# A Mamba-2 scan with a low-rank mixer on one core: 56 TensorE transposes replaced by VectorE 32x32 transposes and a trip through DRAM

## Chip, core and metric

The kernel runs on one core of a Trainium2 chip. The metric is the device time of one execution in microseconds, the median of the runs. The profile is one more execution, taken by the hardware profiler. Its span runs from the first to the last instruction that the profile shows.

## What is computed

Inputs are x (4 batches, 8 heads, 768 steps, 32 channels), the decay a (4, 8, 768), B and C (4, 8, 768, 16), and the mixer's weights U (768 x 32), V (32 x 768), w_ch1 (256 x 1024), w_ch2 (1024 x 256). The reference, cut:

```python
for c in range(nc):                       # chunks of 32 steps
    cum = np.cumsum(la, axis=-1)          # la = log of the decays of the chunk
    L = np.exp(cum[..., :, None] - cum[..., None, :]) * causal
    M = np.einsum('bhin,bhjn->bhij', Cc, Bc) * L
    y_intra = np.einsum('bhij,bhjd->bhid', M, xc)
    y_inter = np.einsum('bhin,bhnd->bhid', Cc, state) * np.exp(cum)[..., None]
    y[:, :, sl] = y_intra + y_inter
    state = decay_full * state + sum over j of Bc[j] xc[j] decay_from_j[j]
x = y.transpose(0, 2, 1, 3).reshape(B, S, H * D)     # (4, 768, 256)
h = x.transpose(0, 2, 1) @ U @ V
u = x + h.transpose(0, 2, 1)
out = u + np.maximum(u @ w_ch1, 0.0) @ w_ch2
```

## The kernel before

The scan works on pairs k = 0 to 11 of two chunks of 128 steps; three pairs make a batch. The mixer works on blocks j = 0 to 2 of 256 steps of a batch. The order of all work is written out by hand: the string PLANS[1] holds words, and `follow` emits each word's instructions in turn, so every engine runs its own instructions in the order of the words. Engines wait for one another through semaphores alone. All DMAs are issued by SyncE (SP), also in order.

Words of the scan, with pair 3 + n for the word's number n (so T3 is pair 6, the first of batch 2, and t6 to t8 are batch 3):

- L loads B, C and x. P (`prep`) scales B and C on VectorE. D (`decayed`) scales B for the states.
- T (`turned`, which runs `turning`) transposes B and C: four TensorE transposes of 128x128 (L497) into one PSUM bank w, then three ACT operations: a copy to T (L501) and two masked copies to Cm (L507). A pair has two T words, each with two of the transposes.
- g (`gram`) multiplies Cm and T (L529), m and M mask the result on VectorE, s (`state`) makes the chunks' states (L564), u (`update`) chains them on VectorE and copies them masked to Sm on ACT (L596).
- n (`intra`, L684) and i (`inter`, L659) make y, channels by steps, in four PSUM banks; y (`yout`) copies it to yT in six ACT operations.
- t (`ytokens`) transposes y back to steps by channels: four TensorE transposes (L714) and a copy to ytok, on ACT for batches 0 and 1, on VectorE for 2 and 3.

Words of the mixer, with the lag of the batch first (p1 is batch 0, p0 batch 1, p-1 batch 2, p-2 batch 3):

- p (`project`, L748) multiplies ytok by U, x (`mixed`, L760) multiplies by V, and a (`added`) adds the result to yT on VectorE, which makes u. Batch 3's p-2 waits for t8, and all of batch 3's mixing waits for p-2.
- S (`split`) splits a block of u in three parts of the type fp32r: one ACT operation and two VectorE ones. f and e (L812 to 831) are the first matmul's two passes with a scaling and a Relu on ACT; h (`third`) makes two more parts on VectorE. R (`refined`) splits the weights in the same manner.
- d (`piece`) is one piece, four matmuls of 128x256, of the second matmul of a block. `down` adds u on VectorE at the end and stores the block: batches 1 to 3 by one VectorE transpose of 128x512 in 32x32 squares and four DMAs that put the squares where they belong (L907 to 912), batch 0 by four TensorE transposes (L920), an ACT copy and one DMA. Batch 3's last block goes through `rows`, whose u is transposed at its start by four TensorE transposes and one ACT copy (L848, L850), while its matmuls give steps by channels right away.

PSUM holds 2 banks w, 3 x and 3 z. A word that needs a bank waits until the bank's last reader is done.

Of the kernel before, what the change touches and what calls it, by code (L numbers as in the profile page):

```python
# [10 lines left out]
FP32 = mybir.dt.float32  # L11
# [3 lines left out]
WCOLS = 512  # L15
NWORDS = 12
PLAIN = 2
ROWS = 3
FOUR = 3

# [3 lines left out]
AF = mybir.ActivationFunctionType  # L24
# [19 lines left out]
        'U1.0.0 g0 U1.0.1 g1 m0 M0 c5 c4 m1 M1 c5 D1 s0 u0 U1.1.0 U1.1.1 U1.1.2 i0 n0 y0 c6 c6 '  # L44
        's1 c5 g2 c7 u1 R2 m2 c7 U1.1.3 M2 c8 c8 c7 U1.0.2 L4 U1.0.3 i1 n1 y1 c6 R1 R0 c8 R5 c9 '
        's2 c9 c9 n2 d1.0 L5 R6 u2 R0 d1.1 P3 S1.2 d1.0 R7 d1.0 i2 y2 R3 t1 R1 t0 R2 R5 d1.1 R4 '
        'f1.2.0 D4 T3 T3 P4 R7 R6 t2 f1.2.1 R3 D3 d1.1 f1.2.2 d1.0 R4 e1.2.0 d1.1 h1.2.0 e1.2.1 '
        'T4 f1.2.3 d1.0 T4 e1.2.2 e1.2.3 h1.2.1 P5 g3 p0 m3 M3 L6 d1.2 d1.2 d1.2 T5 L7 d1.2 L8 '
        'T5 h1.2.2 x0 h1.2.3 d1.2 a0.0 d1.2 d1.2 a0.1 S0.0 d1.2 g4 m4 s3 f0.0.1 D5 M4 f0.0.0 '
        'd1.2 d1.2 d1.2 e0.0.0 e0.0.1 u3 h0.0.0 f0.0.2 d1.2 h0.0.1 f0.0.3 e0.0.2 s4 u4 n3 h0.0.2 '  # L50
        'i3 e0.0.3 h0.0.3 d1.1 D6 S0.1 d1.2 d0.0 d0.0 y3 d0.0 d0.0 d0.0 S0.2 d0.0 d0.0 d0.0 D7 '
        'n4 s5 i4 d0.0 d0.0 g5 P7 y4 u5 P6 m5 M5 d0.0 d0.0 t3 D8 f0.2.1 f0.1.2 s6 n5 i5 y5 '
        'e0.1.2 u6 f0.2.0 f0.1.0 f0.1.3 h0.1.2 T7 e0.2.0 h0.2.0 e0.2.1 e0.1.3 h0.2.1 P8 T7 '
        'h0.1.3 f0.1.1 d0.2 f0.2.2 f0.2.3 e0.1.0 h0.1.0 e0.1.1 h0.1.1 e0.2.2 e0.2.3 h0.2.3 d0.1 '
        'd0.1 T6 T6 d0.1 d0.1 d0.1 t4 h0.2.2 t5 d0.1 d0.1 d0.1 d0.2 d0.2 d0.2 d0.2 d0.0 g7 m7 '
        'p-1 d0.2 d0.2 x-1 M7 a-1.0 a-1.1 s7 d0.2 u7 d0.1 d0.1 d0.1 g6 m6 d0.1 M6 d0.1 d0.2 d0.2 '
        'd0.2 d0.2 d0.2 S-1.0 T8 T8 i6 n6 y6 s8 n7 S-1.1 i7 y7 f-1.0.2 f-1.0.3 g8 e-1.0.2 '
        'e-1.0.3 m8 M8 f-1.1.0 f-1.0.1 h-1.0.3 h-1.0.2 f-1.0.0 f-1.1.1 e-1.1.0 e-1.0.0 e-1.0.1 '
        'h-1.1.0 h-1.0.1 e-1.1.1 f-1.1.2 h-1.0.0 d-1.0 S-1.2 f-1.1.3 e-1.1.2 h-1.1.2 d-1.0 d-1.0 '
        'd-1.0 d-1.0 f-1.2.0 u8 d-1.0 d-1.0 h-1.1.1 d-1.1 e-1.2.0 h-1.2.0 t6 e-1.1.3 f-1.2.2 '  # L60
        'd-1.1 d-1.1 d-1.0 h-1.1.3 e-1.2.2 h-1.2.2 d-1.1 d-1.1 d-1.1 d-1.1 d-1.1 i8 n8 t7 d-1.1 '
        'd-1.1 y8 d-1.1 t8 p-2 d-1.1 x-2 d-1.0 d-1.0 a-2.0 f-1.2.1 a-2.1 S-2.0 d-1.0 d-1.0 S-2.1 '
        'f-1.2.3 e-1.2.1 h-1.2.1 f-2.0.2 e-1.2.3 f-2.0.0 f-2.0.1 d-1.2 d-1.2 e-2.0.0 h-1.2.3 '
        'e-2.0.2 h-2.0.0 f-2.0.3 S-2.2 h-2.0.2 d-1.2 e-2.0.1 d-1.2 d-1.2 d-1.2 e-2.0.3 h-2.0.3 '
        'f-2.1.0 h-2.0.1 f-2.1.1 f-2.1.2 e-2.1.0 e-2.1.1 h-2.1.0 f-2.1.3 d-1.2 d-1.2 d-1.1 '
        'e-2.1.2 h-2.1.1 f-2.2.1 e-2.1.3 d-2.0 d-1.2 d-1.2 d-2.0 d-2.0 d-2.0 h-2.1.2 d-1.2 d-1.2 '
        'd-2.1 d-2.1 d-1.0 h-2.1.3 f-2.2.0 f-2.2.2 d-2.0 d-2.0 d-2.0 d-2.0 e-2.2.2 d-2.1 e-2.2.0 '
        'h-2.2.0 d-1.2 h-2.2.2 d-2.0 d-2.0 f-2.2.3 d-2.1 d-2.1 d-2.1 e-2.2.3 d-2.0 d-2.1 d-2.1 '
        'e-2.2.1 h-2.2.3 d-2.0 d-2.2 d-2.2 d-2.2 d-2.0 h-2.2.1 d-2.1 d-2.1 d-2.1 d-2.1 d-2.2 '
        'd-2.1 d-2.2 d-2.2 d-2.2 d-2.2 d-2.2 d-2.2 d-2.2 d-2.2 d-2.2 '),  # L70
}


# [1 line left out]
def kernel(  # L75
# [27 lines left out]
    nc = tc.nc  # L103
    P = 128
    NB, NH, S, D = x.shape
# [7 lines left out]
    NCB = DM // P  # L113
    HS = 2 * P
    VS = S // 2
    W = DF // 4
    NBL = S // HS
# [25 lines left out]
    def bank(tag, *dims):  # L143
        t = psum.tile([P, *dims], FP32, tag=tag, name=tag, bufs=BANKS[tag])
        if fills[0]:
            idle(t if len(dims) == 1 else t.rearrange(
                {2: "p a b -> p (a b)", 3: "p a b c -> p (a b c)"}[len(dims)]), fills[0])
        fills[0] = 0
        return t
# [39 lines left out]
    def hold(load, until):  # L189

        tc.add_manual_dep(load.ins, until.ins.name, mybir.DependencyInfo(
            mybir.DependencyClass.Sync, mybir.DependencyReason.DATA))
# [293 lines left out]
    def turning(k, c=0, n=2, tag="w", engine=None, sooner=False):  # L486

        s = st[k]
        if c == 0:
            s["T"] = att.tile([P, 2, 2, P], FP32, tag="T", name="T", bufs=3)  # L490
            s["Cm"] = att.tile([P, 2, 2, P], FP32, tag="Cm", name="Cm", bufs=3)
        tp = bank(tag, 2, n, P)
        for i in range(2):
            for v in range(n):
                if i or v:
                    yield
                nc.tensor.transpose(out=tp[:, i, v],  # L497
                                    in_=s["BC"][:, i, c + v].rearrange("p h n -> p (h n)"),
                                    identity=ident)
        if sooner or not engine:  # L500
            nc.scalar.copy(out=s["T"][:, :, c:c + n], in_=tp)  # L501
        for i in range(2):
            if engine:
                engine.tensor_scalar(out=s["Cm"][:, i, c:c + n], in0=tp[:, 1],
                                     scalar1=slot[:, i, None], scalar2=None, op0=ALU.mult)
            else:
                nc.scalar.activation(s["Cm"][:, i, c:c + n], tp[:, 1], AF.Copy,  # L507
                                     scale=slot[:, i, None])
        if engine and not sooner:
            nc.scalar.copy(out=s["T"][:, :, c:c + n], in_=tp)  # L510
        yield

    def turn(*args):
        for _ in turning(*args):
            pass
# [215 lines left out]
    def ytokens(*args):  # L731
        for _ in ytokening(*args):
            pass


    def mixer(b):
# [35 lines left out]
        def block(j):  # L772
            return uT[:, :, ts(j, HS)]
# [67 lines left out]
        def rows(j):  # L841

            u = raw.tile([P, 2 * WCOLS], INT32, tag="words", name="words", bufs=NWORDS).bitcast(
                FP32)[:, :HS // P * DM].rearrange("p (k n d) -> p k n d", n=NCB, d=P)
            t = bank("w", HS // P, NCB, P)
            for k in range(HS // P):
                for n in range(NCB):
                    nc.tensor.transpose(out=t[:, k, n], in_=block(j)[:, n, ts(k, P)],  # L848
                                        identity=ident)
            nc.scalar.copy(out=u, in_=t)  # L850
            yield
            o = mix.tile([P, 2 * WCOLS], FP32, tag="o", name="o")
            at = {}
            order = [(0, 0), (0, 1), (1, 0), (1, 1), (0, 2), (1, 2)]
            for k, v in order:
                if not v:
                    at[k] = bank("xz"[k % 2], DM)
                t = at[k]
                for half in range(2):
                    products(t, [(gs[j, m // 2][v][:, m % 2, ts(k, P)], w2[v][:, m])  # L860
                                 for m in range(NQ * half, NQ * half + NQ)], v + half == 0)
                    if v == 1 and half:
                        scaled(t)
                    if v == 2 and half:
                        vector.tensor_tensor(out=o[:, ts(k, DM)], in0=t,
                                             in1=u[:, k].rearrange("p n d -> p (n d)"),
                                             op=ALU.add)
                        nc.sync.dma_start(
                            out=out[b].rearrange("(j k p) m -> j k p m", j=NBL, p=P)[j, k],
                            in_=o[:, ts(k, DM)])  # L870
                    yield

        def down(j):
# [20 lines left out]
            else:  # L894
                for n in range(NCB):
                    for half in range(2):
# [4 lines left out]
                        if n and half:  # L901
                            added_to(t)
                        yield
            if b:
                o = mix.tile([P, 2 * WCOLS], FP32, tag="o", name="o")
                o = o[:, :NCB * HS].rearrange("p (n i) -> p n i", n=NCB)
                vector.transpose(out=o, in_=block(j))  # L907
                for r in range(4):
                    nc.sync.dma_start(
                        out=out[b, ts(j, HS)].rearrange(  # L910
                            "(k t) (n a c) -> a t n k c", t=Q, n=NCB, c=Q)[r],
                        in_=o[ts(r, Q)].rearrange("p n (k c) -> p n k c", c=Q))
                yield
                return
# [56 lines left out]

    def turned(k):

        t = turns.setdefault(k, turning(k))
        for _ in range(2):
            next(t)

    def crossed(k):

# [2 lines left out]
    def ytokens_of(k, v):  # L982
# [3 lines left out]

    scans = dict(P=prep, D=decayed, T=turned, g=gram, s=state, m=lambda k: mask(k, (0, 1)),
                 M=lambda k: mask(k, (2, 3)), u=update, i=lambda k: inter(k, 0), n=intra,
                 j=crossed, y=yout, t=ytokens, L=load, Q=lambda k, c: prep(k, c, 1),
                 E=lambda k, c: decayed(k, c, 1), O=ytokens_of,  # L990
                 V=lambda k, c, v: turn(k, c, 1, "wx"[v // 2 % 2], vector if v % 2 else None, v > 3))
    whole = dict(c=convert, R=refined, A=lambda i: decays(every_batch, "w", [i]),
# [56 lines left out]
```

## Time and profile before

| what | us |
|---|---|
| median of 3 runs (lowest, highest) | 219.41 (219.27, 221.42) |
| the profiled execution, its own time | 219.55 |
| its span | 217.8 |
| TensorE (PE) busy | 205.9 |
| weight loads (PEld) busy | 185.1 |
| VectorE (DVE) busy | 168.3 |
| ScalarE (ACT) busy | 125.0 |
| GpSimd (POOL) busy | 6.6 |

The page gives, for each engine, busy time, share of the span and number of instructions, then the span in 40 equal slices with the busy share of each in tenths. A group of instructions is a line of the kernel, an engine, an operation and the tiles written and read, with busy time and mean duration in ns, and the idle time just before them with what ended it. VectorE's instructions all carry L169, the line of a helper, and are told apart by their tiles. PE is the matmuls, PEld the weight loads that overlap them. A TensorE transpose counts as a matmul.

### The profile page before, as it was taken

To read this page: it belongs to the slowest core of one execution; us is meant where nothing else is said; L and a number is where in the kernel's file an instruction comes from. 1 tells how busy PE (TensorE), PEld (TensorE's weight loads), DVE (VectorE), ACT (ScalarE), POOL (GpSimd) and SP (SyncE) were. 2 spreads that over 40 slices of the span, in tenths; PEclk is the share of its full clock that TensorE was granted. 3 is DMA by queue.
4 is the path that set the end of the run, shared out by engine and by line. 5 is a ranking of instruction groups with operands and counts; after the bars stand their busy time and mean duration, and the time that the engine had idled before them with its cause. 6 is when DMAs were issued, how large, how long until landed. Compare 5 with 4: busy or idle time off the path is not lost.

```text
span 217.8 us, 7530 instructions
## 1 busy us (share of the span) xinstructions
PE 205.9 (95%) x3246; PEld 185.1 (85%) x3246; DVE 168.3 (77%) x349; ACT 125.0 (57%) x287; POOL 6.6 (3%) x22
## 2 busy tenths in 40 slices
PE   7778799999999999999999999979999999999994
PEld 5555586878879998999999988869999899999993
DVE  3398978998899998699858967847994597874871
ACT  3353749479969774368589513667563276635410
POOL 4132100000000000000000000000000000000000
PEclk9999969999999999999999999999999999999999
DMA  5996789986751017406600020330000000033234
GB/s 82 134 159 178 105 123 225 249 147 157 99 73 26 3 50 97 52 16 87 147 6 0 0 40 14 50 54 0 3 0 3 3 2 0 3 48 51 36 60 96
DMA packets 84016, 14.60 MB, mean 67 GB/s; under 512 B 80336, under 2 KB 82192, under 8 KB 83984
## 3 DMA queue, kind: packets, MB, share of 16 engines
q1 hardware_dynamic: 83984, 14.13, 37.0%
q8 instruction: 25, 0.41, 0.9%
q14 instruction: 7, 0.06, 0.1%
HBM read 10.98 MB, written 3.15 MB: 65 GB/s over the span
## 4 chain that ended last, share of the span: by engine, by line
PE 83%; DVE 6%; ACT 3%; SPq 2%; issue 2%; DMA 2%; POOL 1%; DVEq 0%
PE x L791 35%; PE z L791 28%; PE x L529 3%; SPq L195 2%; PE w L497 2%; PE w L748 2%; PE w L714 2%; DMA bc<-in_B_dram 2%; DVE words L169 2%; PE x L760 2%; PE x L684 1%; PE x L659 1%; PE w L564 1%; PE z L684 1%; DVE M L169 1%
## 5 line engine op out<-in xcount | busy, mean ns | idle before, releaser
L169 DVE SCALAR_TENSOR_TENSOR words<-words 128x512 fp32r<-128x512 f32 (+6 forms) x60 | 39.3, 667 | 4.3 <-PE x L791 1.4
L791 PE MATMUL x<-words,w 128*128 128x256 f32 x288 | 38.3, 280 | 0.0
L791 PEld LDWEIGHTS x<-words,w 128*128 128x128 f32 x288 | 34.9, 188 | 1.8 <-issue 1.7
L791 PE MATMUL z<-u,w 128*128 128x256 f32 x240 | 34.0, 280 | 1.3 <-issue 1.3
L791 PE MATMUL x<-u,w 128*128 128x256 f32 x240 | 34.0, 281 | 0.0
L791 PEld LDWEIGHTS z<-u,w 128*128 128x128 f32 x240 | 30.1, 188 | 1.6 <-issue 1.3
L791 PEld LDWEIGHTS x<-u,w 128*128 128x128 f32 x240 | 30.1, 188 | 0.6 <-issue 0.2
L796 ACT ACTIVATE z<-z 128x512 f32<-128x512 f32 (+1 forms) x24 | 13.9, 578 | 18.0 <-PE z L791 18.0
L796 ACT ACTIVATE x<-x 128x512 f32<-128x512 f32 (+1 forms) x27 | 15.4, 574 | 14.5 <-PE x L791 14.3
L169 DVE SCALAR_TENSOR_TENSOR words<-x,words 128x512 fp32r<-128x512 f32 x20 | 13.7, 685 | 10.7 <-ACT words L831 10.5
L791 PE MATMUL z<-words,w 128*128 128x256 f32 x144 | 19.3, 280 | 0.0
L791 PEld LDWEIGHTS z<-words,w 128*128 128x128 f32 x144 | 17.5, 188 | 0.4 <-issue 0.4
L831 ACT ACTIVATE words<-z 128x512 fp32r<-128x512 f32 x20 | 11.8, 601 | 6.1 <-PE x L791 4.3
L831 ACT ACTIVATE words<-x 128x512 fp32r<-128x512 f32 x20 | 11.8, 600 | 4.8 <-PE x L791 4.7
L169 DVE SCALAR_TENSOR_TENSOR words<-z,words 128x512 fp32r<-128x512 f32 x20 | 13.6, 679 | 1.2 <-ACT words L831 1.2
L169 DVE SCALAR_TENSOR_TENSOR S<-S,kept,w 128x64 f32<-128x64 f32 x40 | 11.2, 279 | 1.6
L169 DVE TENSOR_TENSOR BC<-bc,F 128x512 f32<-128x512 f32 (+2 forms) x18 | 8.9, 508 | 4.2 <-DMA bc<-in_B_dram 2.8
L169 DVE TENSOR_TENSOR M<-x,causal 128x256 int32<-128x256 int32 x24 | 9.0, 417 | 3.8 <-PE z L529 3.8
L169 DVE TENSOR_TENSOR yT<-x,yT 128x384 f32<-128x384 f32 (+1 forms) x15 | 9.2, 612 | 3.2 <-PE z L760 3.1
L596 ACT ACTIVATE Sm<-S,slot 128x128 f32<-128x128 f32 (+1 forms) x18 | 6.1, 386 | 9.1 <-DVE S L169 9.1
L529 PE MATMUL x<-Cm,T 32*64 32x128 f32 x192 | 9.4, 307 | 1.7 <-DVE Cm L169 1.7
L659 PE MATMUL z<-T,Sm 32*64 32x64 f32 x180 | 7.7, 239 | 2.1 <-DVE settled L169 2.0
(152 smaller groups left out, 377.5 us busy)
## 6 DMA issues: line engine op xcount, KB each, us to landing
words<-in_moe_w_ch_dram SPq DMA_DIRECT2D x7, 512.0 KB, 5.9
x<-in_x_dram SPq DMA_DIRECT2D x24, 128.0 KB, 3.9
out_dram<-o SPq DMA_DIRECT2D x32, 64.0 KB, 2.2
bc<-in_B_dram SPq DMA_DIRECT2D x24, 64.0 KB, 3.3
bc<-in_C_dram SPq DMA_DIRECT2D x12, 128.0 KB, 3.7
out_dram<-words SPq DMA_DIRECT2D x3, 256.0 KB, 3.2
words<-in_moe_w_ch_dram SPq DMA_DIRECT2D x2, 256.0 KB, 4.8
out_dram<-o SPq DMA_DIRECT2D x2, 128.0 KB, 1.8
```

Of the source, the lines that this page charges most:

```text
L169: self.last = call(*args, **kwargs)
L195: op = nc.sync.dma_start(**kwargs)
L497: nc.tensor.transpose(out=tp[:, i, v], in_=s["BC"][:, i, c + v].rearrange("p h n -> p (h n)"), identity=ident)
L529: nc.tensor.matmul(out=g[r][cols, c], lhsT=s["T"][rows, 0, c, cols], rhs=s["Cm"][rows, :, :, ts(2 * c + p, Q)].rearrange("r v t i -> r v i ...
L596: nc.scalar.activation(s["Sm"][:, sl, v], s["S"][:, sl, ts(v, D)], AF.Copy, scale=slot[:, v, None])
L659: product = nc.tensor.matmul(out=y[r // 2][p][ts(v, H), c], lhsT=own[ts(r, Q)], rhs=s["T"][ts(r, Q), 1, :, ts(2 * c + p, Q)].rearrange("r ...
L684: product = nc.tensor.matmul(out=y[n][p][ts(v, Q), c], lhsT=x_sb[k][half, c, h], rhs=s["M"][half, h // 2, c, h % 2], start=fresh(k, n, p, ...
L714: nc.tensor.transpose(out=t[c][:, c, g], in_=yT[b][:, g, ts(2 * q + c, P)], identity=ident)
L748: nc.tensor.matmul(out=p[ts(n, H)], lhsT=UU[:, c].rearrange("p t r -> p (t r)"), rhs=ytok[b][:, c, ts(n, P)], start=(c == 0), stop=(c == N ...
L791: nc.tensor.matmul(out=t, lhsT=lhsT, rhs=rhs, start=start, stop=True, skip_group_check=True)
L796: nc.scalar.activation(t, t, AF.Copy, scale=1.0 + EPS)
L831: nc.scalar.activation(gs[j, i][0], t, AF.Relu, scale=NEAR)
```

## The change

For pairs 6 to 11 (batches 2 and 3) B and C, y, and for batch 3's last block u, are no longer transposed by TensorE. VectorE transposes the tile in 32x32 squares into a buffer in SBUF (the weights' tile w1f, by turns its four quarters, which is free by then), four DMAs store the squares to DRAM, each 32 partitions in pieces of 128 B, and one DMA loads them back in their right places, four pieces of 512 B to a partition. For T the masked copies Cm then read the loaded T on ACT. The first word of a pair transposes and stores, the second loads (and for T makes Cm), so the order decides how long the trip may take. Batch 0's last block is stored as the other batches' blocks are. The order of the words from T3 on is new; what stands before it is as it was.

```diff
+SQUARED = 6
...
+    def squares(key):
+        n = len(turns_by)
+        turns_by[key] = n
+        t = w1f[n % NQ].rearrange("p c m -> p (c m)")
+        d = nc.dram_tensor(f"squares{n}", [16, Q, 4, Q], FP32, kind="Internal").ap()
+        return t, d
+
+    def send(sq, d):
+        return [nc.sync.dma_start(
+            out=d[:, :, r].rearrange("w x t -> x w t"),
+            in_=sq[ts(r, Q)].rearrange("x (w t) -> x w t", t=Q)) for r in range(4)]
+
+    def fetch(dst, d, sent):
+        op = nc.sync.dma_start(out=dst, in_=d.rearrange("(w g) x a t -> (g x) w (a t)", w=4))
+        for s in sent:
+            hold(op, s)
+
+    def squared(k):
+        s = st[k]
+        s["T"] = att.tile([P, 2, 2, P], FP32, tag="T", name="T", bufs=3)
+        s["Cm"] = att.tile([P, 2, 2, P], FP32, tag="Cm", name="Cm", bufs=3)
+        sq, d = squares(("T", k))
+        vector.transpose(
+            out=sq.rearrange("p (w g t) -> p w g t", g=4, w=4),
+            in_=s["BC"].rearrange("p i c h n -> p (i c) (h n)").rearrange(
+                "p w (g t) -> p w g t", g=4))
+        sent = send(sq, d)
+        yield
+        yield
+        fetch(s["T"].rearrange("p i c t -> p (i c) t"), d, sent)
+        for i in range(2):
+            nc.scalar.activation(s["Cm"][:, i], s["T"][:, 1], AF.Copy, scale=slot[:, i, None])
+        yield
+        yield
+
+    def squaring(k):
+        b, q = pairs[k]
+        sq, d = squares(("y", k))
+        for n in range(NCB):
+            vector.transpose(
+                out=sq.rearrange("p (c n e x) -> p n c e x", e=4, c=2, n=2)[:, n],
+                in_=yT[b][:, n, ts(q, 2 * P)].rearrange("p (c e x) -> p c e x", c=2, e=4))
+        sent = send(sq, d)
+        yield
+        fetch(ytok[b][:, 2 * q:2 * q + 2].rearrange("p c (n t) -> p (c n) t", t=P), d, sent)
+        yield
...  in rows(j), for u
-            t = bank("w", HS // P, NCB, P)
-            for k in range(HS // P):
-                for n in range(NCB):
-                    nc.tensor.transpose(out=t[:, k, n], in_=block(j)[:, n, ts(k, P)],
-                                        identity=ident)
-            nc.scalar.copy(out=u, in_=t)
+            sq, d = squares(("u", j))
+            for n in range(NCB):
+                vector.transpose(
+                    out=sq.rearrange("p (c n e x) -> p n c e x", e=4, c=2, n=2)[:, n],
+                    in_=block(j)[:, n].rearrange("p (c e x) -> p c e x", c=2, e=4))
+            sent = send(sq, d)
+            yield
+            fetch(u.rearrange("p k n d -> p (k n) d"), d, sent)
...  in down(j)
-            if b:
+            if b or j == NBL - 1:
...
-        t = turns.setdefault(k, turning(k))
+        t = turns.setdefault(k, (squared if k >= SQUARED else turning)(k))
...
+    def sided(k):
+        if k < SQUARED:
+            ytokens(k)
+        else:
+            next(sides.setdefault(k, squaring(k)))
```

The new order, at the places that the prediction speaks of:

```
P4 T3 d1.0 f1.2.0 R4 T4 f1.2.2 t2 e1.2.0 f1.2.1 R6 d1.0 d1.1 D3 R3 h1.2.0 P5 d1.1
e1.2.2 f1.2.3 e1.2.1 p0 T3 d1.2 e1.2.3 T4 T5 L6 h1.2.2 h1.2.1 R7 d1.1 x0 a0.0 a0.1 d1.2
h1.2.3 d1.2 d1.2 d1.2 s3 g3 m3 M3 d1.2 d1.2 S0.0 d1.2 g4 m4 M4 ...
... s4 e0.0.1 u3 e0.0.2 e0.0.3 L7 L8 D5 s5 h0.0.0 i3 n3 y3 d0.0 d0.0 u4 h0.0.1 g5 ...
... T6 n4 ... T7 S0.2 ... u6 t5 ... e0.2.1 t3 ... D7 t4 e0.1.0 h0.1.3 e0.1.1 d0.2 d0.2 d0.2
h0.2.0 h0.2.1 T6 d0.2 t3 h0.2.3 h0.1.0 ... h0.2.2 ... h0.1.1 d0.1 t4 T7 d0.0 P8 T8 s7
u7 g6 m6 d0.1 M6 t5 ... s8 u8 n6 i6 y6 p-1 g7 T8 d0.2 x-1 d0.1 m7 M7 n7 a-1.0 a-1.1 S-1.0
i7 y7 g8 f-1.0.2 f-1.0.3 m8 M8 n8 i8 y8 t6 t7 S-1.1 e-1.0.2 h-1.0.2 t6 e-1.0.3 f-1.0.0
f-1.0.1 h-1.0.3 t8 f-1.1.3 e-1.0.0 ... t7 ... t8 d-1.1 p-2 h-1.1.3 d-1.1 x-2 a-2.0 a-2.1 ...
```

## The prediction

> **What bounds the kernel now.** I read the page's busy rows and slices first, then the chain of work that ended last in order of time, then the busy times by stretch, then groups kept apart by shape, then the DMA issues. Busy time and slices:
>
> ```profile
> PE 205.9 (95%) x3246; PEld 185.1 (85%) x3246; DVE 168.3 (77%) x349; ACT 125.0 (57%) x287; POOL 6.6 (3%) x22
> PE   7778799999999999999999999979999999999994
> DVE  3398978998899998699858967847994597874871
> PEclk9999969999999999999999999999999999999999
> ```
>
> TensorE (PE) is busy 95% of the span at nearly full clock, and from the sixth slice on it hardly ever rests. The busy times by stretch (PE, PEld, DVE, ACT in that order after the length) say the same where the change lies, and that VectorE has room on average:
>
> ```profile
> 80.00:96.00 16.00, 16.00 (x287) 14.41 (x274) 13.21 (x29) 8.46 (x18) 0.00 (x0) 1.00 0.44 68
> 112.00:128.00 16.00, 16.00 (x168) 15.75 (x166) 13.03 (x20) 10.85 (x23) 0.00 (x0) 1.00 0.01 2
> 128.00:146.00 18.00, 16.65 (x424) 14.21 (x411) 12.04 (x28) 8.27 (x24) 0.00 (x0) 1.00 0.30 47
> ```
>
> So from about 66 us to the end every microsecond of PE work taken out is a microsecond of time, unless a new wait takes its place. In the chain (start, length, what) the work that goes is on the path; the one pause worth a name is at 142 us, with nothing shown to wait for:
>
> ```profile
> 97.51 0.87 PE w L920 x8
> 121.56 0.44 PE w L497 x4
> 123.38 0.87 PE w L714 x8
> 142.07 1.26 issue
> 206.86 0.44 PE w L848 x4
> ```
>
> The prices of what comes instead, by shape, and the DMAs by size and time to landing:
>
> ```profile
> L169 DVE STREAM_TRANSPOSE o<-yT 128x512 f32<-128x512 f32 x8 | 5.6, 705 | 0.1
> L169 DVE COPY ytok<-w 128x512 f32<-128x512 f32 x6 | 4.1, 685 | 3.1 <-PE w L714 3.1
> L501 ACT COPY T<-w 128x512 f32<-128x512 f32 x9 | 5.3, 592 | 4.7 <-PE w L497 4.5
> out_dram<-o SPq DMA_DIRECT2D x32, 64.0 KB, 2.2
> out_dram<-words SPq DMA_DIRECT2D x3, 256.0 KB, 3.2
> words<-in_moe_w_ch_dram SPq DMA_DIRECT2D x2, 256.0 KB, 4.8
> ```
>
> **What is removed.** PE loses 56 transposes of 128x128: 24 of B and C (T, L497), 24 of y (t, L714), four of batch 3's last block (L848), four of batch 0's (L920). Four stand in the chain for 0.44 us, whoever issues them, so 14 x 0.44 = 6.2 us. ACT loses six copies of T, one of L850, one of L922: 8 x 0.59 = 4.7 us, all off the path. VectorE loses six ytok copies, 6 x 0.685 = 4.1 us.
>
> **What is added.** VectorE gets six transposes of B and C and one of batch 0's last block of the shape 128x512 (0.705 each, 4.9 us), and 14 of 128x256 for y and u. That last shape is not in the trace: half of 0.705 is 0.35, other 128x256 f32 operations on VectorE take 0.42; I take 0.42, 5.9 us. Net 4.9 + 5.9 - 4.1 = 6.7 us more. Over 66.5 to 206 us VectorE is busy 107.7 of 139.5 us; with 6.7 more in 133 it is 86%: no bound over the whole, so what counts is where it falls behind.
>
> There are 13 trips through DRAM: four stores of 64 KB in pieces of 128 B, then one load of 256 KB. The store has the form of out_dram<-o (L909): issued every 0.63 us, landing after 2.2. The load's form is missing; the rows of 256 KB say 3.2 to 4.8, and I take 3.5. SP waits for the stores before the load, so from VectorE's end to the data there are 3 x 0.63 + 2.2 + 3.5 = 7.6 us, and for T another 1.0 us for two masked copies Cm on ACT (0.49 each). SP issues 13 x 5 + 3 = 68 more DMAs, 43 us of its time; it is in order, so a load waits for every store put ahead of it, and for the output stores and the loads L6 to L8.
>
> **Moved work and where it may wait.** I laid the new order out by hand from old time 66.6 on, each engine's words back to back: f 0.91 us, e and d 0.45, p 1.46, g 0.73, n 0.80 on PE; a pair of h, R or S operations 1.33, the rest 0.60 (0.38 for a mask) on VectorE; 0.58 on ACT. Four of the places that matter:
>
> 1. x0 now stands right after d1.1, about 4 us earlier than before, and its last matmul needs the PSUM bank that h1.2.1 frees. VectorE, which ends R5 at 68.85, has P4, T3, T4, T5, R4, R6, R3, h1.2.0, h1.2.2 and two sums ahead of that: 12.2 us, to 81.1. PE has 13.3 us from 66.6, to 79.9: late by 1.2. g3 and g4 follow straight on a0.1 and the masks: 0.8 more. Sum 2.0.
> 2. s5 stands behind u4, which stands behind h0.0.0 on VectorE (0.65), and g5 behind the sixth copy of y3 on ACT (0.8). Sum 1.4.
> 3. In g7, x-1, n7, i7, g8, f-1.0.2 every word needs the one before it through VectorE: x-1 the masks m7 and M7 (0.9), n7 the sums a-1.0 (0.7), g8 a-1.1 and y7 (0.6). Sum 2.2. Before the change about 6 us of d and g stood there.
> 4. e-1.0.0 behind seven copies and scalings on ACT: 0.65.
>
> That makes 6.3 us if every one is met. The trips as I place them arrive with little room: T6 0.6 us before g6, though behind the stores of t5, t3 and t4; t5 just at its use in p-1, since its load stands behind the stores of d0.0 and of T8; T8 2 us before g8; t8 within 1 us of p-2. So I put them at nothing; late they cost what the second rival says. Behind a late T on ACT stand a Relu (e1.2.3), the scaling of d0.2, or S-1.0, and PE needs each soon.
>
> Is 6.3 to be believed? The old order has the same kinds of places (y4 before g5, a-2.0 before S-2.0), and between 66 and 214 us PE has one pause over 0.3 us, that of 142 us. So the bounds are 0 and 6.3; I take 2.5, nearer the rows.
>
> **The sum.** 219.55 (the profiled execution: span 217.8 and 1.75 around it) - 6.2 + 2.5 = 215.9. The median of the runs is 0.14 below the profiled one, so 215.7. The end itself is unchanged: after the last matmul a sum of 0.42 and the store of one row block.
>
> **Rivals.**
>
> *All is covered, and the pause of 142 us goes as well.* 219.4 - 6.2 - 1.3 = 211.9; with half a microsecond left of the new waits, 212.4. For it: one clear pause in 148 us before. Against: nothing says what the pause is.
>
> *VectorE's queue becomes the bound.* All of 6.3 us is met: 219.4 - 6.2 + 6.3 = 219.5, no change. For it: VectorE's net 6.7 us, and stretches such as s7 to T8 before them, where h0.1.3 to T8 is 11 us on VectorE beside 6.5 on PE. Against: slack follows each such stretch. [...]
>
> *The trips come late* (the slower side). One mechanism: stores and load together land 3.0 us later than I took, by the load's upper row (1.3) and by stores delayed behind one another (L909's slowest landing is 4.4, 2.2 over its median). Then g6 waits 2.4, p-1 0.6 more, p-2 2.2, and T3 holds up e1.2.3 and so h1.2.3 for 0.8: 6.0, so 215.7 + 6.0 = 221.7. It decides from about 1.5 us of lateness on, where half of the gain is gone, and is a loss of over 1% from 3. For it: margins under 1 us at three places. Against: 128 B stores of just this form land in 2.2 us in the trace. [...]
>
> *The change does not do what it says:* ruled out for the count, since the built program has 56 TensorE transposes fewer and 21 VectorE ones more.
>
> **How the numbers follow.** Forecast 0.46 (own range 213.5 to 218), all covered 0.21, VectorE bound 0.18, late trips 0.15. A measurement here tells about 1% from no change, 2.2 us: faster is below 217.2, slower above 221.6. Faster: 0.43 of the forecast's 0.46, all of 0.21, 0.03 of VectorE's, 0.67. Slower: 0.10 of the late trips and 0.02 of the rest (a VectorE bound and a late trip together), 0.12. The rest, 0.21, is the same. Range 211.8 to 221.3: below lies about 0.05, above 0.13.
>
> **What would show it.** Right: PE busy near 200 us, VectorE near 175, ACT near 120; a few PE pauses of 0.5 to 1 us at x0, s5, g5, x-1 to g8, ended by VectorE or ACT; squares stores landing near 2.2 us and loads near 3.5. Wrong: PE waits ended by a DMA at g3, g6, g8 or p-2 (late trips); VectorE over 90% between 70 and 140 us with PE pauses beyond 5 us in sum; or a PE row still as unbroken as before (all covered).

## The result: 1.4% faster, and the profile after

| | before | after |
|---|---|---|
| median of 17 runs each (lowest, highest), us | 220.37 (218.07, 221.78) | 216.81 (215.63, 219.33) |
| ratio to before, 95% interval | 1 | 0.9862 (0.9835 to 0.9890) |
| span of the profiled execution, us | 217.8 | 214.9 |

The ratios leave out disturbed executions (one of experiment 4's took 396 us), the medians do not. Of 220.4 us the ratio takes 3.0 us (2.4 to 3.6); the forecast was 3.7 below the time before. The page after, the lines that answer to the busy times, PE's and VectorE's slices and the clock of before:

```profile
PE 202.0 (94%) x3190; PEld 180.3 (84%) x3190; DVE 173.3 (81%) x364; ACT 120.9 (56%) x279; POOL 6.7 (3%) x22
PE   7768779999999999999999999899999999999994
DVE  4389968998989999999799995786995299859941
PEclk9999969999999999999999999999999999999999
```

PE's row is as full as before: the 7 of the 27th slice, the old pause at 142 us, is gone, and the 26th has an 8, where the sequence from g7 on lies. VectorE's row has eights and nines from the seventh slice to the 24th, with one seven; before, it had two sixes and a five there. By stretch (length, then PE, PEld, DVE, ACT, POOL; last the granted clock, the DMA share and GB/s):

```profile
80.00:96.00 16.00, 16.00 (x246) 13.99 (x243) 15.52 (x34) 8.19 (x17) 0.00 (x0) 1.00 0.61 112
96.00:112.00 16.00, 15.54 (x450) 13.92 (x449) 13.92 (x30) 10.06 (x31) 0.00 (x0) 1.00 0.68 97
112.00:128.00 16.00, 16.00 (x196) 15.55 (x195) 15.52 (x30) 10.81 (x23) 0.00 (x0) 1.00 0.64 129
128.00:146.00 18.00, 17.29 (x465) 14.46 (x464) 12.63 (x31) 8.87 (x28) 0.00 (x0) 1.00 0.50 91
```

From 80 to 128 us VectorE works 44.96 of 48 us, 94%, and PE still rests for half a microsecond only. The DMA share of 112 to 128 us, 0.01 before, is 0.64. The trips' prices, by shape and by DMA:

```profile
L170 DVE STREAM_TRANSPOSE w1f<-yT 128x256 f32<-128x256 f32 x14 | 5.2, 416 | 0.0
L170 DVE STREAM_TRANSPOSE w1f<-BC 128x512 f32<-128x512 f32 x6 | 4.2, 707 | 0.1
squares<-w1f SPq DMA_DIRECT2D x52, 64.0 KB, 2.3
T<-squares SPq DMA_DIRECT2D x6, 256.0 KB, 4.4
ytok<-squares SPq DMA_DIRECT2D x6, 256.0 KB, 3.0
```

No PE wait of the profile after is ended by a load of squares: the trips are covered. The largest of the new waits is at x-1. In the order of time (start, length, instruction, and in brackets the idle time before it and what ended it):

```profile
134.14 1.30 DVE L170 STREAM_TRANSPOSE o<-yT 128x512 f32<-128x512 f32 x2
...
135.53 0.27 ACT L761 COPY yT<-x 128x128 f32<-128x128 f32 x1 [0.63 <-DVE o L170]
...
137.09 0.27 ACT L808 COPY pT<-w 128x128 f32<-128x128 f32 x1
137.40 0.59 PE L815 MATMUL x<-V,pT 32*128 32x384 f32 x2 [0.61 <-ACT pT L808]
```

The tile of y of batch 3 takes the place of batch 1's. ACT's copies y6 write it, so they wait until VectorE has turned batch 1's last two blocks for the output (the first line), and pT, which x-1 reads, stands behind the six copies on ACT.

Word by word, the unchanged head ran 1.2 us later in the profile after than in that of before, and the changed part, from the first new word to the end, took 147.0 instead of 151.2 us, 4.2 less. In it: the 56 transposes gone (6.2 by the prediction's price), the pause of 142 us gone (1.4), and 3.4 of new waits: 2.4 in g7 to f-1.0.2 (x-1 1.2, n7 0.5, f-1.0.2 0.7), 0.7 inside n3 (0.44 of it with nothing shown to wait for; in several profiles of the experiments n3 is 0.3 to 0.5 shorter), 0.3 at g3. Most of these waits lie inside PE's records: from the first new word to the last matmul the records leave 1.2 us free, where before they left 1.4.

### The profile page after: what moved, and what is told of

Read it like the earlier page. It is cut to its first block, busy times and chain, and to the rows that moved or that the text cites. A ratio compares the mean times of both kernels' runs of the same rounds, so it can differ in the third digit from the quotient of the medians.

```text
span 214.9 us, 7508 instructions
## 1 busy us (share of the span) xinstructions
PE 202.0 (94%) x3190; PEld 180.3 (84%) x3190; DVE 173.3 (81%) x364; ACT 120.9 (56%) x279; POOL 6.7 (3%) x22
## 4 chain that ended last, share of the span: by engine, by line
PE 80%; SPq 6%; DMA 5%; ACT 3%; DVE 3%; issue 2%; DVEq 0%; ACTq 0%
PE x L846 36%; PE z L846 28%; SPq L196 6%; DMA bc<-in_B_dram 3%; PE x L584 2%; DMA bc<-in_C_dram 2%; PE z L739 2%; PE x L815 2%; PE x L739 2%; PE w L803 1%; PE x L714 1%; ACT yT L759 1%; PE x L803 1%; DVE o L170 1%; PE w L619 1%
## 5 line engine op out<-in xcount | busy, mean ns | idle before, releaser
L846 PE MATMUL z<-u,w 128*128 128x256 f32 x240 | 32.6, 277 | 0.0
L584 PE MATMUL x<-Cm,T 32*64 32x128 f32 x192 | 10.8, 307 | 1.6 <-DVE Cm L170 1.5
```

The source lines that it names most:

```text
L584: nc.tensor.matmul(out=g[r][cols, c], lhsT=s["T"][rows, 0, c, cols], rhs=s["Cm"][rows, :, :, ts(2 * c + p, Q)].rearrange("r v t i -> r v i ...
L846: nc.tensor.matmul(out=t, lhsT=lhsT, rhs=rhs, start=start, stop=True, skip_group_check=True)
```

## Experiments

Times are medians; a difference is taken to the changed kernel, 216.8 us with ratio 0.9862. By the ratios, each taken beside the kernel before, the differences of experiments 1, 2, 3 and 8 are smaller: 9.2, 9.1, 6.2 and 4.2 us. The last group ran beside the changed kernel itself, 217.6 us there.

**1. The order alone.** The new order, with TensorE transposing B, C and y again at each pair's second word:

```diff
-        t = turns.setdefault(k, (squared if k >= SQUARED else turning)(k))
-        for _ in range(2):
+        if k >= SQUARED and k not in turns:
+            turns[k] = turning(k)
+            return
+        t = turns.setdefault(k, turning(k))
+        for _ in range(4 if k >= SQUARED else 2):
...
-        if k < SQUARED:
+        if k < SQUARED or k in sides:
             ytokens(k)
         else:
-            next(sides.setdefault(k, squaring(k)))
+            sides[k] = None
```

> The changed kernel's order, but B, C and y of batches 2 and 3 are turned by TensorE again: 48 of the 56 transposes are back, 12 groups of four, and VectorE has 12 squares' operations' work less (batch 0's last block and batch 3's carried sum stay as in the changed kernel). Main theory (the gain is TensorE's removed work, the new order only makes room for the trips): TensorE busy about 207 us, and about 216.8 + 12 x 0.44 = 222.1 us, the new waits at x-1 and after n3 still there since the order makes them; at most 1 us less where they came from VectorE's squares. Rival (the order alone brings the gain, by filling the pause that stood at 142 us): near 217, no slower than the changed kernel by over 1 us.

227.06 us, ratio 1.0279 (1.0217 to 1.0341): 10.2 us more than with the trips, and slower than before. Both sizes were wrong, and the rival is out. Word by word against the changed kernel, a group of four transposes alone moves PE's row by 0.35 to 0.46 us, as expected; the rest comes in places where an operation of VectorE now stands behind TensorE. The two largest waits of this kind in the waits of the run (engine, line, what ended them, us in all, times, longest), and one of PE that follows from the first:

```profile
DVE ytok L170 <- PE w L769: 5.1, 3, 3.5
DVE BC L170 <- PE w L498: 4.4, 1, 4.4
PE x L846 <- DVE words L170: 1.7, 1, 1.7
```

VectorE's copy of t3 to ytok waits 3.5 us for transposes that the order puts late on PE; h0.2.3, h0.1.0 and h0.2.2 stand behind it in VectorE's queue, and d0.2 waits 1.7 us for them. P5 waits 4.4 us because its tile BC is not free until T3 has been read, so the sums a0.0 and a0.1 and h1.2.3 are late, and PE loses 1.25 us behind x0. The trip takes PE out of these dependencies: VectorE reads BC and y when it comes to them.

**2 and 3. One kind of trip alone.** The two halves of the edit above, first y by TensorE and T by trips, then T by TensorE and y by trips.

> The changed kernel with y of batches 2 and 3 turned by TensorE at the second t word (24 transposes back, copies to ytok on VectorE again); B and C still go through DRAM. Main theory (every group of four transposes is worth its 0.44 us, wherever it stands): 216.8 + 6 x 0.44 = 219.4 us, TensorE busy about 204.6. Rival (t's trips cost waits of their own at p-1 and p-2, so that nothing was won there): 216.8 or less.

> The changed kernel with B and C of batches 2 and 3 turned by TensorE at the second T word (24 transposes and six copies of ScalarE back); y still goes through DRAM. Main theory: 216.8 + 6 x 0.44 = 219.4 us, TensorE busy about 204.6. Rival (T's trips and the 0.7 us operation of VectorE cost what they win, above all between s7 and g8): 216.8 or less.

226.2 us (ratio 1.0274, 1.0206 to 1.0342) and 223.7 us (1.0143, 1.0079 to 1.0207): 9.4 and 6.9 more than with both, where 2.6 each was expected. Neither rival holds, and the losses do not add up to experiment 1's. Run 2 has the waits behind the ytok copy (1.9 us at d0.2, 1.6 after g6), run 3 those behind P5 and at g6 (1.3 and 1.5). In run 2 the granted clock falls as well: 0.62 and 0.53 in two stretches of 4 us, where PE's records show it busy throughout (0.50 from 144.9 to 151.8 us).

```profile
144.00:148.00 4.00, 4.00 (x134) 2.92 (x130) 3.54 (x7) 1.98 (x7) 0.00 (x0) 0.62 0.43 66
148.00:152.00 4.00, 4.00 (x38) 3.54 (x28) 1.42 (x4) 0.91 (x3) 0.00 (x0) 0.53 0.16 26
```

**4. The price of a TensorE group by itself.** In `first`, ahead of 14 of the f words:

```diff
             gs["t", j, i] = t = bank("xz"[i % 2], 2, HS)
+            if b == 2 or b == 3 and j == 0 and i < 2:
+                for m in range(4):
+                    nc.tensor.transpose(out=t[:, m // 2, ts(m % 2, P)], in_=ident, identity=ident)
```

> The changed kernel with 14 groups of four more TensorE transposes (of the identity, into the bank that the f word behind them overwrites at once) ahead of the first 14 f words of batches 2 and 3, in a stretch where TensorE never rests; nothing waits for them and they wait for nothing new. It measures what a group of four is worth on the path. Prediction's term: 14 x 0.44 = 6.2 us, so 223.0 us. By the steps of the run with the new order and TensorE's transposes (0.35 to 0.46 each): 14 x 0.37 = 5.2, 222.0 us. Rival (TensorE's work is partly covered by the waits that follow): below 219 us.

222.1 us, ratio 1.0071 (1.0035 to 1.0108). In the trace PE falls back by 0.35 to 0.47 us at each of the 14 groups, 6.1 us from n7 to the end. The ratios say 4.6 us more than the changed kernel (0.0209 of 220.4; 3.6 to 5.6 with the two half-widths added as squares), the medians 5.3. So a group on the path is worth 0.33 to 0.44 us; the prediction's 0.44 is the upper end, and the rival is out.

**5. Late trips.** Each load twice, the second after the first:

```diff
-        op = nc.sync.dma_start(out=dst, in_=d.rearrange("(w g) x a t -> (g x) w (a t)", w=4))
+        src = d.rearrange("(w g) x a t -> (g x) w (a t)", w=4)
+        first = nc.sync.dma_start(out=dst, in_=src)
         for s in sent:
-            hold(op, s)
+            hold(first, s)
+        op = nc.sync.dma_start(out=dst, in_=src)
+        hold(op, first)
```

> Each of the 13 loads from DRAM is done twice, the second after the first has landed, so that all data come about 3 to 4.4 us later and SP stands that much longer before what is behind it. By the prediction's price (3.0 us late: g6 2.4, p-1 0.6, p-2 2.2, T3 0.8) about 6 us more than the changed kernel, 222.8 us, with TensorE's waits at g6 (its data came 0.9 us before use), p-1 and p-2 (2.2 us before use). Rival (the trips have more room than the margins say, since words behind them can be taken up by the slack of ScalarE): at most 1.5 us more, below 218.3.

243.74 us, ratio 1.1051 (1.0987 to 1.1114): 26.9 us more, over four times the prediction's price. The waits of the run (engine and line, what ended them, us in all, times, longest; SPq is SP's queue), and two stretches of it:

```profile
PE z L849 <- ACT z L854: 9.6, 1, 9.6
ACT Cm L554 <- DMA T<-squares: 26.6, 6, 11.3
SPq L536 <- DMA T<-squares: 18.2, 6, 4.2
SPq L536 <- DMA ytok<-squares: 18.0, 6, 4.4
140.00:144.00 4.00, 0.00 (x0) 0.00 (x0) 0.00 (x0) 0.09 (x1) 0.00 (x0) 0.50 0.53 129
144.00:148.00 4.00, 2.07 (x9) 2.07 (x10) 0.00 (x0) 1.88 (x5) 0.00 (x0) 0.50 0.64 107
```

The lateness is not 4 us each time: SP waits in order for each first load, and each delay is handed to the words behind it, so T6 lands 6.6 us later than in the changed kernel, t3 11, T7 17, where PE itself was 4.4 late ahead of them. ACT stands behind T7's Cm for 11.3 us, the scaling of d0.1 (L854) behind that, and PE waits 9.6 us for the scaling, a word that has nothing to do with T7. Then the clock is at 0.50 (the last two lines), and PE's 3190 matmuls take 210.2 us instead of 202.0.

**6. One late trip.** The same for T8's load alone (`k == 11`):

> The changed kernel with one load alone done twice, T8's, so that T of pair 11 comes about 4 us later (142 instead of 138.1 us); all else is in time. Prediction's price for a late trip (lateness less the margin of its own matmuls): Cm ends at 143 instead of 139.0, g8 stood at 140.1, so 2.9 us more, 219.7 us. Second theory (ScalarE stands in order behind the late T: the split S-1.0 and the six copies of y7 wait for the two masked copies, and g8 and f-1.0.2 wait for those): y7's copies end at 146, so 4 to 5 us more, 221 to 222 us, and more if TensorE's clock falls in the pause as it did after the pauses of the runs with doubled loads and with the old order. Third (only the series of all 13 trips on SP made those runs slow): within 1 us of 216.8.

220.36 us, ratio 1.0016 (0.9977 to 1.0055), beside 217.59 and 0.9889 for the changed kernel in the same group: 2.8 us more. T8 came 2.2 us late, g8 started 1.2 us later (2.2 less about 1.1 of margin, the first theory's rule), g8 itself took 0.5 us longer (0.19 of it a wait for y7's copies) and f-1.0.2 0.8, since the clock fell (0.50 from 140.8 to 144.2 us). PE in the stretch of g8, with and without the late load:

```profile
140.00:144.00 4.00, 3.50 (x40) 2.88 (x41) 3.08 (x8) 2.13 (x8) 0.00 (x0) 0.60 0.49 75
140.00:144.00 4.00, 3.90 (x119) 3.25 (x108) 3.97 (x11) 2.33 (x9) 0.00 (x0) 1.00 0.35 53
```

So the total is what the first theory said (2.9), but of two halves, margin and clock; the copies of y7 cost 0.2 us and not the second theory's 2, and the third theory is out, since one late trip alone costs time.

**7. The trips in the old order.** The plan of before, with each y's (and u's) send and load in its one word and T's two words as they stood (`T5 d1.2 T5 L7 L8` in place of `T5 L7 d1.2 L8 T5`):

```diff
-            next(sides.setdefault(k, squaring(k)))
+            for _ in squaring(k):
+                pass
```

> The kernel before, in its old order of words, with the same trips through DRAM in place of TensorE's transposes: each t word and batch 3's u store and load at once, T's two words as they stood (T5's second word one place earlier, ahead of L7). Main theory (the reorder is there to hide the trips, 7.6 us each and 1.0 us for Cm): T8 stands about 6 us before g8, t5 about 6 us before p-1, t8 right before p-2, so TensorE waits about 3 + 2 + 8 us and more where ScalarE stands behind a late T: 220.4 - 6.2 + 13 = about 227 us or more, with waits ended by the DMAs of squares. Rival (the order is of no matter to the trips): 214.2 us.

282.13 us, ratio 1.2781 (1.2712 to 1.2850): 62 us slower than before, where 7 was expected. The sign was right, the size far off, for the reasons of experiment 5. Its waits, and the clock in four neighbouring stretches:

```profile
ACT Cm L551 <- DMA T<-squares: 49.1, 6, 13.8
PE w L803 <- DMA ytok<-squares: 19.5, 5, 7.1
PE x L739 <- ACT yT L761: 12.3, 2, 11.7
150.00:156.00 6.00, 0.00 (x0) 0.00 (x0) 0.64 (x2) 1.39 (x3) 0.00 (x0) 0.78 0.54 122
156.00:162.00 6.00, 1.74 (x14) 1.34 (x16) 0.00 (x0) 0.00 (x0) 0.00 (x0) 0.50 0.68 132
162.00:168.00 6.00, 6.00 (x64) 4.20 (x61) 1.88 (x5) 0.70 (x2) 0.00 (x0) 0.58 0.07 11
168.00:174.00 6.00, 5.72 (x180) 4.99 (x179) 5.39 (x14) 1.36 (x4) 0.00 (x0) 1.00 0.06 11
```

PE rests 61.7 of 278.9 us and is busy 217.2 us with the work that took 202.0; how much of these 15 us is the half clock after the pauses, and how much waits inside the records, is not separated. The reorder is not an extra to the trips; without it they lose twenty times what they win.

**8. More for VectorE.** Each of T's and y's transpositions twice (for T the instruction repeated, for y `for n in (0, 1, 0, 1)`):

> Each of the 13 VectorE squares' operations of T, and each pair of them of y, is done twice (u's not): 6 x 0.705 + 6 x 0.76 = 8.8 us more of VectorE, nothing else changed, so VectorE busy near 182 us. Main theory (VectorE's queue has slack after each full stretch and bounds only a few places): the operations before T7, T8, t5 to t8 push VectorE's next words by 0.7 to 1.5 us each, TensorE waits for a part of it, 1 to 3 us, 218 to 220 us. Rival (VectorE's queue is the bound, so what is put on it is paid in full): 216.8 + 8.8 = 225.6 us. Second rival (VectorE is covered throughout): within 0.5 us of 216.8.

222.29 us, ratio 1.0054 (1.0016 to 1.0091): 5.5 us more (4.2 by the ratios), between the expectation (1 to 3) and the rival (8.8). In the trace 2.2 us are lost at e1.2.1 and behind x0, for the 2.1 us that T3 to T5 add; 1.9 us at f0.2.2 and f0.1.1 of 3.7 us for T6, T7 and t3 to t5; 0.6 at f-1.1.2. Between 70 and 128 us, then, what is put on VectorE in these two places is half to wholly paid.

**9. Less for VectorE.** The scalings D of batches 1 to 3 on GpSimd, as batch 0's are:

```diff
-        (vector if b else nc.gpsimd).tensor_tensor(
+        nc.gpsimd.tensor_tensor(
```

> The changed kernel, but the nine scalings of B for the states (D, 128x256, 0.41 us each on VectorE, batches 1 to 3) are done by GpSimd, which does the same for batch 0 in 0.70 us and is idle otherwise. VectorE loses 3.7 us, 2.5 of them between 70 and 116 us where it is 94% busy. If VectorE bounds that stretch (the run with doubled squares paid 5.5 of 8.8 us), 1 to 2 us less: about 215.3 us. Rival (VectorE has slack there): no change, 216.8 us. Second rival (GpSimd is late with D4 or slows VectorE): slower than 217.5.

218.11 us, ratio 0.9921 (0.9887 to 0.9955), beside 217.59 and 0.9889 (0.9845 to 0.9933): no gain. The operation takes 0.76 us there. Word by word the part from D3 on takes the same time to 0.1 us. In it 0.4 us is won at g3 and n3 and lost again at n7, after p-1 has waited 0.9 us for the load of t5, which pushed g7 and its masks back. With experiment 8 this suggests that VectorE stands just under the bound, so that more is paid and less wins nothing; that less can win nothing is not shown, since a late trip took back what this profile had won.

**10. The wait at x-1.** Batch 1's last blocks are turned for the output right behind their sums, and stored where they were (a `yield` between the two in `down`):

```diff
                 vector.transpose(out=o, in_=block(j))
+                if b == 1 and j:
+                    yield
...
-t5 d0.1 d0.2 d0.1 d0.2 d0.2 d0.2 d0.1 d0.1 d0.1 d0.1 s8 u8 n6 i6 y6
+t5 d0.1 d0.2 d0.1 d0.2 d0.2 d0.2 d0.2 d0.1 d0.1 d0.1 d0.1 s8 u8 d0.1 n6 i6 y6
```

> The changed kernel, but batch 1's last two blocks are turned on VectorE right behind their sums (block 2 before block 1's sum, block 1 behind u8), while their stores stay where they are in SP's order. Reading of the changed kernel's trace: x-1 waits behind y6, and y6 waits until VectorE has turned these two blocks (135.44 us), since the tile of y of batch 3 takes the place of batch 1's. Then y6 begins about 0.5 us earlier, x-1 too, and the time is about 216.3 us. Rival (the prediction's step: x-1 waits for the masks of g7): no gain, 216.8 us.

216.33 us, ratio 0.9794 (0.9747 to 0.9841). In the trace, y6 no longer waits for the transposition but starts as soon as ACT has done u8's copies, and x-1 starts at 137.12 us, 0.6 earlier against the words before it:

```profile
134.46 0.70 DVE L170 STREAM_TRANSPOSE o<-yT 128x512 f32<-128x512 f32 x1
134.58 0.64 ACT L651 ACTIVATE Sm<-S,slot 128x96 f32<-128x96 f32 x2 [4.21 <-DVE S L170]
135.25 0.27 ACT L761 COPY yT<-x 128x128 f32<-128x128 f32 x1
```

That confirms the chain for x-1's start; the masks, which the prediction named, end only a wait of the last weight loads of x-1 (0.25 us in the changed kernel, 0.36 here). The time is 0.5 us below the changed kernel's, as expected (1.5 by the ratios), but the two intervals overlap, so a gain in time is likely and not shown.

**11 and 12. The changed kernel again, and both edits together.**

> The changed kernel itself, beside the three others on the same chip: 216.8 us, as before. It is the measure for them.

> Both together: batch 1's last two blocks turned right behind their sums, and the scalings D on GpSimd. If both gains are real and stand at different places they add: 216.8 - 0.5 - 1.5 = 214.8 us. If neither is: 216.8 us.

The changed kernel: 217.59 us, ratio 0.9889 (0.9845 to 0.9933). Both edits: 217.36 us, 0.9844 (0.9783 to 0.9906), not told apart from it. x-1 comes 0.7 us earlier in the trace, as in experiment 10, and n7 takes 0.3 of it back; from D3 on the trace is 0.9 us shorter than that of the changed kernel. The best candidate is experiment 10's kernel; none beats the changed one beyond the intervals.

## The prediction, step by step

- **Removed, 14 x 0.44 = 6.2 us: right, perhaps a little high.** Experiment 4 gives 6.1 us in its trace and 4.6 to 5.3 in its times.
- **VectorE net 6.7, near 175: measured 173.3, 5.0 more.** The prices were right (0.416 for the 0.42 taken, 0.707 for 0.705): the durations of the added operations sum to 10.8 us, and less the six copies (4.1) to the 6.7. Busy time counts covered time once, and records of operations in a row overlap by up to 0.1 us (the 14 of 0.416 us sum to 5.8 us and are 5.2 us busy), so it rose by 5.0 only. ACT came to 120.9 (120), PE to 202.0 (200): PE's busy time does not fall by the chain's 6.2, only by 3.9, since most of the new waits lie inside its records.
- **The trips at nothing: right in this order.** Stores landed in 2.3 us (2.2 taken), loads of ytok in 3.0 and of T in 4.4 (3.5 taken). T8's trip took 10.65 us from VectorE's end to the data, not 7.6: its stores stood 1.4 us behind d0.0's on SP, and its load landed in 4.9; it still had 1.1 us before g8. The load of t5 was as close to its use as the prediction laid out: in the profiles of experiments 6 and 9 p-1 waits 0.3 and 0.9 us for it.
- **New waits, 2.5 of 6.3: the net was 2.0, but made of other parts.** 3.4 us of waits came and 1.4 went, since the pause of 142 us, which the forecast kept, is gone. That 2.0 lies so near the 2.5, a choice between 0 and 6.3, is luck. Place by place: x0, g3, g4 were put at 2.0 and cost 0.3; s5 and g5 at 1.4 and cost nothing of their own, while n3 beside them lost 0.7; g7 to f-1.0.2 at 2.2 and cost 2.4; e-1.0.0 at 0.65 and cost nothing. The laid-out VectorE queue was too long before x0 and right at the one place where every word needs the one before it.
- **The cause at x-1 was wrong:** it starts late not for masks m7 and M7 but for the tile shared by two batches, as experiment 10 shows.
- **Rival "all is covered":** its pause of 142 us went, and PE's row is as unbroken as before, which the prediction had named as a sign of being wrong. Yet 3.4 us of waits came, inside the records, and the time is 4.4 us above this rival's 212.4: an unbroken row of busy tenths did not show that all is covered. What the pause was stays open.
- **Rival "VectorE becomes the bound":** not in this kernel, but nearer than "86%" over 133 us said. From 70 to 140 us VectorE is at 90% while PE rests 1.1 us only; the stretch from 80 to 128 us has 94%, and experiment 8 pays 4.2 to 5.5 of 8.8 us.
- **Rival "late trips", 6.0 us for 3 us late: the mechanism right, its price wrong.** Its 3.0 us is itself less than the 1.3 and 2.2 that it is put down to. The term that failed added up four margins as if each trip were late by itself. With one trip late (experiment 6) margin arithmetic holds for g8; with all of them late (experiment 5) SP adds up the delays, ACT blocks other words behind Cm (11.3 us at T7), and the clock falls (0.50 from 140 to 148 us): 26.9 us.

## What to carry to other kernels

Moving work from the bounding engine to a detour paid here only where the order gave each trip its time; cost the trips and the order as one change, since either alone lost more (ratios 1.0279 and 1.2781) than both won (0.9862). With every load late the delays in the in-order queues were not priced by their margins (26.9 us in experiment 5, where margins gave about 6): follow what stands behind the waiting instruction on SP and on ACT, and add up the delays along the queue. Look at an engine's load by stretches of some 16 us: an average of 84% hid one of 94%, where extra work was paid by half or more (experiment 8).

## What the runs showed of the hardware

- **Half clock after short pauses.** In experiment 6 PE rested less than 1 us at a time, 1.9 us in the 6.6 before 140.8 us (0.29, 0.61 and 0.96), and the granted clock was 0.50 from there to 144.2 us; the changed kernel rests 0.7 us at the same place and keeps 1.00. Experiments 5 and 7 show the same 0.50, in stretches where PE rests 5.9 of 8 us (140 to 148 us) and 4.3 of 6 us (156 to 162 us). There the clock is 1.00 again from 152 to 156 and from 168 to 174 us, behind 4 and 6 us in which PE is busy throughout; in experiment 6 it came back 3.2 us after PE's last rest. No length of pause decides it in these runs: experiment 2's clock fell at 144.9 us after a single rest of 0.6 us in 8, while experiment 9's kept 1.00 after one of 0.9, so what sets it off stays open.
- **PE 4% slower with the clock shown as 1.00.** In some stretches pieces of d follow each other every 0.47 us instead of every 0.45, while DVE and ACT operations of 128x512 keep their durations (692 and 583 ns in the changed kernel and in its repeated run). In the repeated run of the changed kernel and in experiment 6 this lasts from about 155 us to the end, in experiments 1 and 2 from about 175; other profiles have shorter stretches of it (the changed kernel's from 128 to 132 us). From 156 to 211 us it makes 1.9 us. Its cause stays open.
- **The head varies too:** the first T0 transposes started at 29.97 and at 32.48 us in two profiles of the same kernel. The words before were 1.1 us later in the second, and there the granted clock was 0.50 from 28.9 to 32.3 us, where the first has 1.00. The head and the 4% are together of the size of the spread of nearly 4 us between runs, and single traces differ from the medians by 1 us here; that they make the spread is not shown.
